# Retention and channel mix on one core: q scaled while it is turned, y copied mostly by ScalarE, 64-token chunks everywhere, a new order

## The chip, the cores and the metric

The kernel runs on one core of one Trainium2 chip. The metric is device time in microseconds (us) of one execution; a result is the median over several runs. The engines are TensorE (PE in the profile; its weight loads are PEld), VectorE (DVE), ScalarE (ACT), GpSimd (POOL) and SyncE (SP); the last three also issue DMAs. Matmuls write PSUM, which has 8 banks of 512 fp32 columns for each of 128 partitions; the other memory on the chip is SBUF.

## What is computed

Two layers, one behind the other. The first is a retention layer over 4 sequences of 768 tokens, with 8 heads of 64 columns; the second mixes each token with the one before it and puts it through two projections and a gate.

```python
gamma = 1.0 - 2.0 ** (-5.0 - np.arange(H))
for t in range(S):
    state = gamma * state + outer(k[t], v[t])        # per batch and head, 64 x 64
    y[t] = (1 / sqrt(D)) * q[t] @ state
...
x = y, heads side by side                            # [4, 768, 512]
xk = mu_k * x + (1 - mu_k) * x_prev
xr = mu_r * x + (1 - mu_r) * x_prev
k = np.maximum(xk @ w_k, 0.0)                        # 512 -> 1024
v = k * k @ w_v                                      # 1024 -> 512
r = sigmoid(xr @ w_r)
out = r * v
```

Inputs and outputs are fp32; the matmuls take fp16.

## The kernel before

The 3,072 tokens are cut into 12 blocks of 256 (three for each sequence). The recurrence is done in chunks: inside a chunk the scores q k are masked and multiplied with v, and what came before the chunk enters through a carried state of 64x64 per head. The powers of gamma are split: `vs` multiplies v by one power as it becomes fp16 (`scale_v`, L280), and the block's y is multiplied by the matching inverse powers, held in the tile `gy`, when it is read from PSUM (`yout`, L573 and L580). `gy` is built on the chip at the start (`powers`).

The work is written out by hand as one long string, `ORDER`: one word for each step, and each engine runs its steps in that order. A word has a code, the block, a part, behind `~` the engine (v VectorE, a ScalarE, p GpSimd, s SyncE) and behind `@` the PSUM banks. In order of the data the codes are:

- `lq`, `lk`, `lv`: loads of a block. Those of GpSimd turn q and k into fp16 on the way. The first heads of block 0 come through SyncE as fp32 and are turned into fp16 by ScalarE (`cq`, `ck`). `wk`, `wr`, `wv` load the weights, `mu` the mixing factors.
- `Tq`, `Tk`: transposes on PE into PSUM; `Eq`, `Ek`: ScalarE copies the transposed blocks to SBUF (L265). For blocks 9 to 11, `tq` and `tk` do both as a transposing DMA on SyncE instead.
- `S`, `M`: scores, and their mask on VectorE (L420). `C`: the chunk's addition to the state; `U`: VectorE adds it to the carried state (L485); `G`: the state decays over to the next block. `I` and `J`: q times the carried state; `Y`: the masked scores times `vs`, into the same banks.
- `D`: y from PSUM to the fp32 tile `xT` (VectorE); `dx`: its difference to the token before (L595); `X`: the two mixes (L621), four column groups each.
- `K`: keys (L635, L645); `Qa`, `Qb`: relu (L667) and square (L675, L679), both on ScalarE; `R`, `s`: gate and sigmoid; `V`: values (L700), in two halves of their sum; `O`: result on VectorE (L706); `st`: store, issued by SyncE. The last half block's values are cut in two (`Vc`, L718; `Oc`, L725).
- `z`: products of zeros on PE, which only fill time at the start.

Attention is done in three ways. Blocks 0 and 1 use chunks of 128 tokens with two tokens interleaved in a row; blocks 2 to 5 (`WIDE`) use chunks of 128 tokens with 128 rows of one chunk; blocks 6 to 11 (`HALF`) use four chunks of 64 tokens, whose products are all 64x64x64, four of them side by side on the array. Blocks 3 to 5 and 9 to 11 load q and k as whole pairs of heads (`PAIRQ`, `PAIRK`), so that one 128x128 transpose turns two heads. Blocks 3 and 4, 6 and 7, 9 and 10 are joint (`GROUPS`): their keys are products of 512 columns (L635), those of the others of 256 (L645).

Tiles come in rings (four of q, k and v; three of `vs`, of the transposed q and k and of the mixes; four of relu outputs), so a step may also wait until a buffer's last reader is done.

## Time and profile before

| what | us |
|---|---|
| runs | 153.79, 364.5, 154.08 |
| median of the runs | 154.08 |
| span of the profiled execution | 152.4 |
| PE busy | 145.3 |
| VectorE busy | 128.0 |
| ScalarE busy | 94.5 |
| GpSimd busy (issuing loads) | 62.1 |

The profile is one execution, taken by the hardware profiler; its span goes from the first to the last instruction, and the execution's own time is somewhat longer: the median of the runs is 1.7 us above this span (the profiled execution's own time isn't among the runs, which are timed without a profile). Durations of single instructions overlap on PE, where the next matmul starts before the last one has ended, so on PE the distance between two starts is the better measure. In a group of instructions the columns are the line, the engine, the operation, output and inputs with shapes, the count, busy time and mean duration in ns, and then the engine's idle time in front of them with what ended it. In a timeline they are the start, the time taken, the engine, the line and the operation.

### The profile page before, as it was taken

The numbers are of one execution on the slowest core, as the hardware profiler recorded it, in microseconds if no ns is written. First come the engines' busy times: TensorE is split into PE (matmuls) and PEld (weight loads), VectorE is DVE, ScalarE is ACT, GpSimd is POOL, SyncE is SP. The second block draws the span as 40 slices with busy tenths as digits, with TensorE's granted clock in tenths as the row PEclk, the third lists the DMA queues.
The fourth block names the chain that finished last, engine by engine and source line by source line (L and its number), as shares of the span: only waits on it lengthen the run. The fifth ranks groups of instructions, "written<-read, shape, count | busy, mean of one in ns | idle before, by whom it ended". The sixth has DMA issues, their size and how long they took to land.

```text
span 152.4 us, 4956 instructions
## 1 busy us (share of the span) xinstructions
PE 145.3 (95%) x2129; PEld 82.4 (54%) x2129; DVE 128.0 (84%) x204; ACT 94.5 (62%) x172; POOL 62.1 (41%) x77
## 2 busy tenths in 40 slices
PE   7969899999999999999999999999999999999991
PEld 3345467657864545545448544447664444466460
DVE  2289999999999999999999998998999999331651
ACT  3655259979955679966418807869450089739430
POOL 7965658999746920599989000000000000000000
PEclk9999999999999999999999999999999999999999
DMA  5999999999999999299999999928103013003153
GB/s 146 237 241 192 181 240 237 148 148 223 167 178 216 213 225 286 68 239 166 258 188 238 236 168 126 152 89 109 38 4 138 0 71 142 0 0 138 69 207 138
DMA packets 56525, 23.83 MB, mean 156 GB/s; under 512 B 48056, under 2 KB 52024, under 8 KB 56504
## 3 DMA queue, kind: packets, MB, share of 16 engines
q0 software_dynamic: 45200, 14.95, 82.1%
q1 hardware_dynamic: 10872, 8.26, 22.3%
q8 instruction: 16, 0.26, 0.7%
q10 hardware_dynamic: 432, 0.32, 0.7%
q14 instruction: 5, 0.04, 0.1%
HBM read 24.31 MB, written 6.29 MB: 201 GB/s over the span
## 4 chain that ended last, share of the span: by engine, by line
PE 73%; DVE 11%; DMA 11%; issue 2%; ACT 0%; DVEq 0%; POOLq 0%
PE ps L700 24%; PE ps L688 14%; PE ps L635 12%; PE ps L645 11%; DMA kT<-k 6%; DMA v<-in_v_dram 5%; DVE a L420 3%; PE ps L507 2%; PE ps L311 2%; DVE xk L621 2%; DVE xT L580 2%; DVE dx L595 2%; PE ps L544 1%; DVE vs L280 1%; PE ps L388 1%
## 5 line engine op out<-in xcount | busy, mean ns | idle before, releaser
L700 PE MATMUL ps<-wv,k2s 128*128 128x512 f16 x184 | 43.9, 380 | 0.0
L667 ACT ACTIVATE kr<-ps 128x512 f32<-128x512 f32 x48 | 27.9, 594 | 23.0 <-PE ps L635 14.9
L700 PEld LDWEIGHTS <-k2s 128*128 128x128 f16 x184 | 17.2, 98 | 19.0
L706 DVE SCALAR_TENSOR_TENSOR os<-ps,rs 128x512 f32<-128x512 f32 x23 | 15.2, 684 | 12.1 <-PE ps L700 6.5
L688 PE MATMUL ps<-wr,xr 128*128 128x512 f16 x96 | 24.0, 379 | 0.0
L259 POOL DMA_DIRECT2D v<-in_v_dram x20 | 18.0, 911 | 13.6 <-DVE vs L280 8.3
L645 PE MATMUL ps<-xk,wk 128*128 128x256 f16 x192 | 23.4, 273 | 0.0
L635 PE MATMUL ps<-xk,wk 128*128 128x512 f16 x96 | 22.8, 379 | 0.0
L420 DVE TENSOR_TENSOR a<-ps,c_sb 128x1024 f16<-128x1024 f32 (+1 forms) x20 | 21.9, 1110 | 0.0
L694 ACT ACTIVATE rs<-ps 128x512 f32<-128x512 f32 x24 | 14.3, 594 | 10.6 <-PE ps L688 8.8
L645 PEld LDWEIGHTS <-wk 128*128 128x128 f16 x192 | 18.2, 98 | 3.9
L621 DVE SCALAR_TENSOR_TENSOR xr<-dx,mu,xT 128x256 f16<-128x256 f32 (+1 forms) x36 | 19.3, 566 | 0.0
L621 DVE SCALAR_TENSOR_TENSOR xk<-dx,mu,xT 128x256 f16<-128x256 f32 (+1 forms) x36 | 18.9, 569 | 0.3
L259 POOL DMA_DIRECT2D k<-in_k_dram x20 | 17.7, 896 | 3.5 <-DMA wv<-in_moe_w_v_dram 1.6
L280 DVE TENSOR_TENSOR vs<-v,csm_sb 128x1024 f16<-128x1024 f32 x12 | 14.5, 1217 | 3.3 <-DMA v<-in_v_dram 3.3
L675 ACT ACTIVATE k2s<-kr 128x512 f16<-128x512 f32 x24 | 14.7, 626 | 0.4
L595 DVE TENSOR_TENSOR dx<-xT 128x1024 f32<-128x1024 f32 x12 | 14.6, 1221 | 0.2
L635 PEld LDWEIGHTS <-wk 128*128 128x128 f16 x96 | 9.1, 98 | 10.5 <-issue 0.2
L679 ACT ACTIVATE k2s<-kr 128x512 f16<-128x512 f32 x24 | 14.5, 625 | 0.3
L688 PEld LDWEIGHTS <-xr 128*128 128x128 f16 x96 | 9.0, 98 | 10.0
L265 ACT COPY qT<-ps 128x1024 f16<-128x1024 f16 (+1 forms) x10 | 9.2, 924 | 7.7 <-PE ps L317 3.7
L265 ACT COPY kT<-ps 128x1024 f16<-128x1024 f16 (+1 forms) x10 | 9.3, 934 | 6.9 <-PE ps L306 3.4
(73 smaller groups left out, 151.3 us busy)
## 6 DMA issues: line engine op xcount, KB each, us to landing
out_dram<-os SPq DMA_DIRECT2D x23, 256.0 KB, 3.8
v<-in_v_dram POOLq DMA_DIRECT2D x20, 256.0 KB, 6.8
k<-in_k_dram POOLq DMA_DIRECT2D x21, 128.0 KB, 6.9
q<-in_q_dram POOLq DMA_DIRECT2D x13, 128.0 KB, 7.1
q<-in_q_dram POOLq DMA_DIRECT2D x5, 256.0 KB, 9.0
v<-in_v_dram POOLq DMA_DIRECT2D x2, 512.0 KB, 7.3
wv<-in_moe_w_v_dram POOLq DMA_DIRECT2D x2, 512.0 KB, 9.5
wk<-in_moe_w_k_dram POOLq DMA_DIRECT2D x2, 256.0 KB, 9.6
```

Source lines behind the costliest of these rows:

```text
L259: e.dma_start(out=to[:, i, hs], in_=src[:, i])
L265: e.copy(out=out, in_=in_)
L280: e.tensor_tensor(out=VS(n), in0=V32(n).rearrange("p (h i d) -> p i h d", i=2, h=H), in1=gks[:, int(half(n) or wide(n)), :, :, None].to_br ...
L420: nc.vector.tensor_tensor(out=dst, in0=dst if n in SPLITM else src, in1=mask[:, None, None, :].to_broadcast(list(dst.shape)), op=ALU.mult,)
L595: e.tensor_tensor(out=DX(k)[:, :, m * TM + t0 : m * TM + t1], in0=x[:, :, c + t0 : c + t1], in1=x[:, :, c - 1 + t0 : c - 1 + t1], op=ALU.s ...
L621: nc.vector.scalar_tensor_tensor(out=XM[w](k)[:, j, t0:t1], in0=DX(k)[:, j, t0:t1], scalar=mu[:, w * NCO + j : w * NCO + j + 1], in1=x[:, ...
L635: nc.tensor.matmul(banks("K", n, g), lhsT=wk16[:, co, g * P : g * P + P], rhs=XM[0](k)[:, co, :], start=(co == 0), stop=(co == NCO - 1),)
L645: nc.tensor.matmul(pz[:, i, :], lhsT=wk16[:, co, fo * P : fo * P + P], rhs=XM[0](k)[:, co, m * TM + t0 : m * TM + t1], start=(i == 0 and c ...
L667: nc.scalar.activation(out=kr, in_=banks("K", n, g, *u), func=AF.Relu)
L688: nc.tensor.matmul(banks("R", n, tb), lhsT=XM[1](k)[:, co, t : t + P], rhs=wr16[:, co, :], start=(co == 0), stop=(co == NCO - 1),)
L700: nc.tensor.matmul(banks("V", n, tb), lhsT=K2(n)[:, fo, tb * P : tb * P + P], rhs=wv16[:, fo, :], start=(fo == 0), stop=(fo == NFO - 1),)
L706: nc.vector.scalar_tensor_tensor(out=OS(2 * n + tb), in0=banks("V", n, tb), scalar=1.0 / (KSC * KSC), in1=RS(2 * n + tb), op0=ALU.mult, op ...
```

## The change

All blocks now use 64-token chunks (`HALF` for all of them; the other two ways and the flags that chose them are gone), so each state has four parts and each block four `U`. The mask has one form. Each k and v is loaded with a chunk's tokens in one row range (two DMAs for each block), each q with two neighbouring tokens in a row. No block is transposed by DMA any more.

The powers of gamma move from y to q: `tu` builds, once, an identity matrix of 64 rows for each head and token parity, scaled by the inverse powers (`scaled_eye`), and q is turned by a matmul with it instead of by a transpose; its PSUM output is fp32 and takes two banks. k is turned by 64x64 transposes. With that, y needs only a constant factor, and `yout` is a copy with a factor: ScalarE does it for most blocks, VectorE for the whole of blocks 5, 8 and 9 and half of blocks 0 and 1. `gy` and `powers` are gone. For seven blocks ScalarE reads two columns of the banks in question (`sy`, `settle`) between `I` and `Y`.

Of 48 squares, 18 go from ScalarE to GpSimd; of 12 scalings of v, 7 go from VectorE to GpSimd, of 12 differences 3 (blocks 3, 7 and 11), and one state decay. The loads of v of blocks 4 to 11 go from GpSimd's queue to SyncE's. The order of all steps is new: at the start, q of block 0 is loaded first on SyncE as before, v of block 0 before the rest of k and q on GpSimd, the first half of `wk` before the second; two of block 0's four key groups come before the scores of block 1, and all but the last half of the values of blocks 0 and 1 come before the transposes of block 3.

```diff
 KSC = 64.0
-KUP = 4.0
-HALF = (6, 7, 8, 9, 10, 11)
-PAIRQ = (3, 4, 5, 9, 10, 11)
-PAIRK = (3, 4, 5, 9, 10, 11)
-WIDE = (2, 3, 4, 5)
-DT = (9, 10, 11)
+YSC = 0.125 * KSC
+DT = ()
...
-gy.0 lq.0.0.2~s lk.0.0.2~s mu~s cq.0.0.2~a lv.0~p z.8@7 Tq.0.0.2@0 ck.0.0.2~a vs.0~v Eq.0.0.2~a
...
+lq.0.0.2~s lk.0.0.2~s lv.0~p mu~s lk.0.2.4~p cq.0.0.2~a tu.0.4~v tu.4.8~v z.11@7 Tq.0.0.2@01
+lq.0.2.4~p ck.0.0.2~a Eq.0.0.2~a z.1@7 Tk.0.0.2@23 lv.1~p Ek.0.0.2~a z.1@7 S.0.0.2@45 M.0.0.2
+lq.1~p vs.0~v z.2@7 mt@6 me~a wk.0 z.1@3 Tk.0.2.4@07 C.0@12 Ek.0.2.4~a U.0.0~v U.0.1~v z.1@6
+Tq.0.2.4@34 lk.1~p U.0.2~v Eq.0.2.4~a U.0.3~v S.0.2.4@56 I.0@07 G.0~a M.0.2.4 sy.0~a wk.1 Y.0
+D.0.1~v D.0.0~a dx.0~v z.2@6 Tq.1@34 Eq.1~a vs.1~p X.0.0.0 X.0.0.3 X.0.0.1 X.0.0.2 wr X.0.1.3
+z.7@6 K.0.0@1 X.0.1.0 X.0.1.2 K.0.1@2 X.0.1.1 Qa.0.0~a lk.2~p Qb.0.0~a C.1@56 Tk.1@07 Qa.0.1~a
+U.1.0~v Ek.1~a U.1.1~v U.1.2~v Qb.0.1~a I.1@34 U.1.3~v S.1@12 G.1~v K.0.2@0 lq.2~p M.1 K.0.3@7
+lv.2~p Qa.0.2~a Y.1 Qa.0.3~a D.1.0~v D.1.1~a R.0.1@5 wv.0 Qb.0.3~a dx.1~v wv.1 R.0.0@6 s.0.1
+Qb.0.2~p X.1.0.3 Tk.2@12 s.0.0 X.1.0.0 Ek.2~a X.1.0.1 lk.3~p X.1.0.2 Tq.2@07 X.1.1.2 K.1.3@3
+X.1.1.3 Eq.2~a X.1.1.0 K.1.1@4 lq.3~p X.1.1.1 Qa.1.3~a R.1.0@5 Qb.1.3~a vs.2~p Qa.1.1~a K.1.0@6
+s.1.0 Qb.1.1~a S.2@12 lv.3~p C.2@07 Qa.1.0~a M.2 K.1.2@3 V.0.1.0@4 U.2.0~v Qa.1.2~a lk.4~p U.2.1~v
+R.1.1@5 Qb.1.2~a U.2.2~v I.2@16 s.1.1 sy.2~a V.0.1.1 lq.4~p Y.2 Qb.1.0~p lv.4~s O.0.1 V.0.0.0@2
...
+Y.11 s.10.1 V.9.1.0@7 D.11~a V.10.1.0@2 dx.11~p V.9.0.0@6 V.10.0.0@0 X.11.1.2 V.9.0.1 X.11.0.2
+X.11.0.3 V.10.1.1 X.11.0.0 O.9.0 V.9.1.1 O.10.1 V.10.0.1 X.11.0.1 st.10.1~s O.9.1 K.11.1@3 O.10.0
...
+    gk_np = gam[None, None, :] ** (C - tok[:, :, None])
+    gq_np = gam[None, None, :] ** (tok_q[:, :, None] - C)
...
+    def scaled_eye(e, h0, h1):
+        hs = slice(h0, h1)
+        e.tensor_tensor(
+            out=turn[:, :, hs], in0=ident[:, None, None, :].to_broadcast([P, 2, h1 - h0, W]),
+            in1=gqs[:, :, hs, None].to_broadcast([P, 2, h1 - h0, W]), op=ALU.mult,
+        )
...
+    def trans_q(e, n, j0=0, j1=NJ):
+        src = held_as(n, 0)
+        pt = turned(n, 0, j0, j1)
+        for j in range(j0, j1):
+            for i in range(2):
+                for u in range(2):
+                    for s, h, hp in heads(j):
+                        nc.tensor.matmul(
+                            pt[low(s), u, j - j0, i], lhsT=src[low(u), i, h],
+                            rhs=turn[low(u), i, h], start=(j == j0 and i == 0),
+                            stop=(j == j1 - 1 and i == 1), skip_group_check=True,
+                        )
...
+    def settle(e, n):
+        copy(e, seen[low(0)], banks("I", n)[low(0), 0, NJ * C - 2 :])
...
-            for v in range(2):
-                nc.vector.tensor_tensor(
-                    out=x[:, :, :, v],
-                    in0=banks("I", n)[:, v].rearrange("p (j i t) -> p j i t", j=NJ, i=2),
-                    in1=g[:, :, :, v], op=ALU.mult,
-                )
+        for u in range(2) if v is None else (v,):
+            if e is nc.scalar:
+                e.activation(out=x[:, u], in_=y[:, u], func=AF.Copy, scale=YSC)
+            else:
+                e.tensor_scalar(out=x[:, u], in0=y[:, u], scalar1=YSC, scalar2=None, op0=ALU.mult)
...
+        if e is nc.scalar:
+            e.activation(out=to, in_=kr, func=AF.Square)
+        else:
+            e.tensor_tensor(out=to, in0=kr, in1=kr, op=ALU.mult)
...
     def store(e, n, tb):
-        nc.sync.dma_start(out=out[b, t0 : t0 + P, :], in_=OS(2 * n + tb))
+        e.dma_start(out=out[b, t0 : t0 + P, :], in_=OS(2 * n + tb))
```

## The prediction

> **What bounds the kernel now.** I read the page's busy times first, then its strip of 40 slices, then the groups by line.

> ```profile
> PE 145.3 (95%) x2129; PEld 82.4 (54%) x2129; DVE 128.0 (84%) x204; ACT 94.5 (62%) x172; POOL 62.1 (41%) x77
> ...
> PE   7969899999999999999999999999999999999991
> ...
> DVE  2289999999999999999999998998999999331651
> ```

> A TensorE (PE) at 95% may be matmuls that wait inside, so I checked it by count: the large projections (keys L645 and L635, gate L688, values L700 and L718), how many there are, and how far apart two of them start in a dense stretch.

> ```profile
> L700 PE MATMUL ps<-wv,k2s 128*128 128x512 f16 x184 | 43.9, 380 | 0.0
> ...
> L688 PE MATMUL ps<-wr,xr 128*128 128x512 f16 x96 | 24.0, 379 | 0.0
> L645 PE MATMUL ps<-xk,wk 128*128 128x256 f16 x192 | 23.4, 273 | 0.0
> L635 PE MATMUL ps<-xk,wk 128*128 128x512 f16 x96 | 22.8, 379 | 0.0
> ```

> ```profile
> 75.27 3.45 PE ps L700 x16
> ...
> 135.16 1.75 PE ps L645 x16
> ...
> 147.29 1.76 PE ps L718 x16
> 149.07 0.42 DVE os L725
> ```

> In the chain of waits, 16 products of 512 columns take 3.45 us (0.2155 each) and 16 of 256 take 1.75 (0.109). So the projections need (184 + 96 + 96) x 0.2155 + (192 + 16) x 0.109 = 81.0 + 22.7 = 103.7 us, and the change alters neither their number nor their shape. The first starts here, in the timeline:

> ```profile
> 20.78 1.09 PE L645 MATMUL ps<-xk,wk 128*128 128x256 f16 x8
> ```

> The last ends at 147.29 + 1.76 = 149.05. Of these 128.3 us, 103.7 are projections; 24.6 are left for all attention products in between and for idleness. To see which, take one run of attention products between projections:

> ```profile
> 69.55 1.03 PE L688 MATMUL ps<-wr,xr 128*128 128x512 f16 x4
> 70.50 0.45 PE L432 MATMUL ps<-vs,k 64*64 64x64 f16 x32
> 70.86 0.45 PE L375 MATMUL ps<-qT,kT 64*64 64x64 f16 x32
> 71.11 0.45 PE L528 MATMUL ps<-a,vs 64*64 64x64 f16 x32
> 71.39 0.32 PE L507 MATMUL ps<-qT,tg 64*64 64x64 f16 x12
> 71.65 1.04 PE L700 MATMUL ps<-wv,k2s 128*128 128x512 f16 x4
> ```

> From 69.55 to 71.65, less 4 x 0.2155, is 1.24 us for 108 products of 64x64x64: 11.5 ns each, the changes to and from the small tiles included. The chain also names a DMA (a transposed load of k, 6% of the span) near 86 us, but that is no hole:

> ```profile
> 86.00:120.00 34.00, 33.57 (x565) 18.22 (x564) 32.18 (x51) 18.20 (x33) 0.00 (x0) 1.00 0.75 103
> ```

> PE is busy 33.57 of those 34.00 us at the full clock. So before 20.78 us VectorE (DVE) and the loads set the pace, and after it PE does, with hardly a gap. The time is: first projection 20.8 + projections 103.7 + small products 24.6 + tail 3.3 (149.1 to the span's end, 152.4) = 152.4. Around the span lies what the runs show beyond it: 154.08 (their median) less 152.4, 1.7 us; the lowest run, 153.79, would make it 1.4. The profiled execution's own time is not among them, so I sum to its span and add 1.7.

> **The change on PE.** From the first projection on, the new order leaves for block 1 all but its q transposes (160 products) and for blocks 2 to 11 all six stages: 5 x 32 + 32 = 192 products each. Less the states and carried terms that first and last blocks of a sequence leave out (32 + 24), that is 2,024 products x 11.5 ns = 23.3 us. Before, the same stretch cost 24.6 with every gap in it. Blocks 2 to 5 get cheaper (16 products with 128 rows or columns become 32 small ones; 8 whole-pair transposes become 32), blocks 9 to 11 get transposes that were DMA transposes before. Turning q by a matmul with a scaled identity, with fp32 output, isn't in the trace; its nearest rows are the 64x64x64 products above, so I keep 11.5 ns. The run above is a long one, and short ones pay the change of tiles more often; so I take the mean of 23.3 and 24.6, 23.9, and keep 23.2 to 25.3 as ends (the upper one if q's products, 22 x 16 of the 2,024, took 15 ns). The new 64-token chunks are thus almost a wash; the time hangs on when the first projection starts (t0) and on the idle time (g) that the new order puts behind it: time = t0 + g + 103.7 + 23.9 + 3.3 + 1.7 = **t0 + g + 132.6**.

> **The change on VectorE, ScalarE, GpSimd.**

> ```profile
> L420 DVE TENSOR_TENSOR a<-ps,c_sb 128x1024 f16<-128x1024 f32 x16 | 19.2, 1217 | 0.0
> ...
> L595 DVE TENSOR_TENSOR dx<-xT 128x1024 f32<-128x1024 f32 x12 | 14.6, 1221 | 0.2
> L280 DVE TENSOR_TENSOR vs<-v,csm_sb 128x1024 f16<-128x1024 f32 x12 | 14.5, 1217 | 3.3 <-DMA v<-in_v_dram 3.3
> ...
> L621 DVE SCALAR_TENSOR_TENSOR xk<-dx,mu,xT 128x256 f16<-128x256 f32 x24 | 10.4, 480 | 0.2
> ...
> L485 DVE TENSOR_TENSOR tg<-ps,tg 128x256 f16<-128x256 f32 x20 | 8.4, 420 | 0.6 <-PE ps L432 0.3
> L573 DVE TENSOR_TENSOR xT<-ps,gy_sb 128x512 f32<-128x512 f32 x12 | 8.3, 689 | 0.7
> ```

> VectorE loses 7 of 12 scalings of v (-8.5 us), five whole masks and two of half size (-7.5), 16 of 24 half-blocks of y (-10: 12 x 0.689 and six whole ones at 1.22, less 8 x 0.689), 3 differences (-3.7) and the short powers of gamma; it gains 15 state sums at 0.42 (+6.3) and two halves of a scaled identity (+1.4, sized like half a copy of y): 128 becomes about 105.

> ```profile
> L667 ACT ACTIVATE kr<-ps 128x512 f32<-128x512 f32 x48 | 27.9, 594 | 23.0 <-PE ps L635 14.9 <-PE ps L645 7.9
> ...
> L675 ACT ACTIVATE k2s<-kr 128x512 f16<-128x512 f32 x24 | 14.7, 626 | 0.4
> ...
> L265 ACT COPY qT<-ps 128x1024 f16<-128x1024 f16 x8 | 8.1, 1010 | 7.2 <-PE ps L306 3.4 <-PE ps L317 3.2 <-PE ps L311 0.6
> ...
> L858 POOL MEMSET const-float32-0.0<- 128x1 f32 x1 | 0.1, 99 | 0.2 <-issue 0.2
> ...
> L750 DVE MEMSET warm<- 128x1 f32 x1 | 0.1, 59 | 0.0
> ```

> ScalarE (ACT) gives 18 squares away (-11.3), takes 16 half-blocks of y (0.59 each by the relu's row, +9.5) and six more transposed copies (+6.1), loses two blocks' state scalings and the powers, and gets seven two-column reads (`sy`) that wait for a block's carried products; behind such a read stand relus, and PE would wait for their banks. About 94.5 + 4.3 = 99 at most, 65% of the span, so I put the hidden cost at nothing (rival 3 prices it without cover).

> GpSimd (POOL) only issues loads now, so the length of its arithmetic is in no row. Below, it is as fast as VectorE (1.22 us for v, 0.6 for a square); the only pair of like rows, two one-column memsets, is 99 against 59 ns, a factor 1.7; I take 2.1 us and 1.1, and three times VectorE (3.7) as the upper end. It gets 7 v, 18 squares, 3 differences and a scaling, 40 to 45 us, and gives 16 loads of v to SP. There they stand behind stores, each of which waits for a result on VectorE; who would wait is the scaling of that block's v, blocks later. I cost that at nothing. [...]

> **t0.** The start is a chain; its steps stand in the timeline:

> ```profile
> 8.30 1.23 DVE L280 TENSOR_TENSOR vs<-v,csm_sb 128x1024 f16<-128x1024 f32 x1 [3.27 <-DMA v<-in_v_dram]
> ...
> 9.57 0.45 PE L461 MATMUL ps<-vs,k 64*64 64x64 f16 x32 [0.27 <-DVE vs L280]
> ...
> 12.84 0.64 PE L555 MATMUL ps<-a,vs 64*64 64x128 f16 x32
> ...
> 13.74 1.22 DVE L580 TENSOR_TENSOR xT<-ps,gy_sb 128x1024 f32<-128x1024 f32 x1
> ...
> 15.00 1.23 DVE L595 TENSOR_TENSOR dx<-xT 128x1024 f32<-128x1024 f32 x1
> ...
> 16.34 0.48 DVE L621 SCALAR_TENSOR_TENSOR xk<-dx,mu,xT 128x256 f16<-128x256 f32 x1
> ```

> Now block 0's difference is ready at 16.2, but block 1's masks and sums come between it and the mixes, so the first projection waits until 20.78. In the new order: v is scaled from about 8.5 (the mask of the first heads goes before it) to 9.7; state 0.45; four sums 1.7, so 11.9; last mask 0.69, 12.6; products to the start of the copy 0.9, 13.5; half a copy 0.69, the other half on ScalarE, 14.2; difference 1.23, 15.5; four mixes at 0.42 (a queue of them runs at that pace), 17.2. PE follows them one by one: **t0 = 17.0**, 3.8 earlier. v now comes in two halves with shorter rows; that may cost up to 1 us or nothing.

> **g.** From there VectorE needs four more mixes (18.9), four sums (20.6), a scaling and mask (22.2), products 0.9 (23.1), half a copy (23.8), difference (25.0), four mixes: 26.7. In these 9.7 us PE has four key groups (8 x 0.109 each: 3.5), two gates (1.7) and 224 small products (160 of block 1, 64 of block 2's transposes: 2.6), 7.8 in all: **1.9 idle**. Next, the second half of wv:

> ```profile
> POOL wk L741 <- DMA q<-in_q_dram: 1.6, 2, 0.8
> ...
> v<-in_v_dram POOLq DMA_DIRECT2D x20, 256.0 KB, 6.8
> ...
> wv<-in_moe_w_v_dram POOLq DMA_DIRECT2D x2, 512.0 KB, 9.5
> ```

> It stands behind 25 loads on GpSimd's queue at some 0.8 us (20), one scaling of v (2.1), and waits of which the quoted one is the longest kind (about 3), from 1.3 on: issued near 26.5, landed at 33.3 with v's 6.8 or at 36 with its own 9.5. PE wants it after two key and gate sets of block 1 (3.5 + 1.7), two stages of block 2 (0.7) and half a value group (0.9): 26.7 + 6.8 = 33.5. So 0 to 2.5 idle; I take **0.5**, nearer to v's, since by then fewer loads queue ahead of it. At the end, block 11's difference is on GpSimd: copy 1.2, difference 2.1, five mixes and two results 3.5, against eight half value groups (32 x 0.2155 = 6.9) on PE: with the steps from engine to engine **0.5** idle. The middle has cover, since VectorE has 23 us less to do; I put 0 there. g = 2.9, and t0 + g + 132.6 = **152.5 us**, 1% under 154.1: t0 + g is 19.9 where it was 20.8, and the small products give 0.7. This case covers 151.2 (v on time, wv free: t0 + g 18.6) to 155.5 (t0 1 us and wv 2 us later).

> **Rivals.** (1) PE is dense from its first projection on: t0 16.3 (v on time, first mixes overlapped), g 1.0: 149.9, 2.7% faster. For it: PE before shows no gaps, and VectorE is eased everywhere. Against: the 1.9 of idle counted above is VectorE's own chain. (2) GpSimd's arithmetic and VectorE's two-input work hold each other up. The place is the start: v of block 1 is due on GpSimd at about 14 to 16, just when the difference and mixes of block 0 run, and a square and v of block 2 at 24 to 30, on the mixes of block 1. If one excludes the other, 2.1 + 1.1 + 2.1 = 5.3 fall on that chain: g 8.2, so 17.0 + 8.2 + 132.6 = 157.8, 2.5% slower; at the upper end of 3.7 for each v it would be 161. It decides once GpSimd takes over 2.5 us for a v or VectorE stands still during it. Of the trace before nothing speaks for or against: GpSimd did no arithmetic. [...] (3) ScalarE in order: a copy of y waits for its products in front of relus that hold PSUM banks, so PE stalls for banks, 0.59 for each of 14 half copies in the middle if nothing covers them, 8 us: 152.5 + 8 = 160.5. That ScalarE stands idle for 38% of the span now, most of it waiting for PE, speaks against it. (4) The change doesn't do what it says, for instance GpSimd's squares come so late that values wait; priced like (3).

> **How the numbers follow.** My case 0.42; rival 1, 0.33; rival 2, 0.17; rivals 3 and 4 together 0.08. What a measurement of this kernel can tell from no change is about 2%, 3.1 us: faster means under 151.0, slower over 157.2. My case lies within; rival 1 is faster; 2 to 4 are slower. The range runs from rival 1 with a little more (149.0: t0 16.0, g 0.4) to rival 2 (157.8).

> **What would show it.** Right: first projection near 17, VectorE at about 104 us busy, GpSimd's v near 2 us, PE idle in 17 to 36 about 3 us and hardly later. Wrong: mixes (0.48) or differences (1.22) that grow longer beside GpSimd's work, PE waiting for relus or for vs after 40 us, or attention products above 11.5 ns each, which at 13 would add 2,024 x 1.5 ns, 3 us.

## The result, and the profile after

The change made the kernel slower: 198.9 us (195.6 to 202.2, 4 runs) against 154.4 beside it, 1.272 times as long (95% interval 1.263 to 1.281). Two of these four runs are slow ones (201.2 and 202.2 us at a mean clock of 0.909 and 0.898, the others 195.6 and 196.5 at 0.925 and 0.939); the ratios to the kernel before, here and below, leave such runs out, so 1.272 is less than the quotient of the two medians. The span of the profiled execution is 194.8 us at a mean clock of 0.939, where it was 152.4 at 1.000. On the page after the change, the busy times and two rows of the strip of 40 slices:

```profile
PE 154.3 (79%) x2845; PEld 85.0 (44%) x2845; DVE 113.4 (58%) x186; ACT 96.9 (50%) x169; POOL 88.6 (46%) x88
...
PE   7576959389976837978677766799789988799991
...
PEclk9955888859999999999999999699999999999999
```

TensorE (PE) has holes from end to end, and its granted clock is a half from 10.4 to 20.7 us and again from 27.5 to 30.9, 37.7 to 44.6 and 123.1 to 126.5. To see where the time went, I gave each matmul the time to the next one's start, less the idle time that the trace lists in front of the next one (0.15 us and over). For the kernel before, the change, and four of the kernels below:

| us | first projection | idle after it | projections | small products, filling zeros | last matmul starts |
|---|---|---|---|---|---|
| before | 20.8 | 0.6 | 106.6 | 20.8 | 148.8 |
| after | 21.6 | 29.9 | 115.1 | 23.9 | 190.5 |
| e1_again | 23.2 | 14.2 | 110.8 | 24.3 | 172.5 |
| e8_spread | 22.4 | 13.0 | 110.2 | 23.5 | 169.2 |
| e12_loads | 21.5 | 13.3 | 111.4 | 25.9 | 172.1 |
| e14_vs_v | 19.7 | 6.3 | 110.5 | 29.5 | 166.0 |

Of the 41.7 us between before and after, 29.3 are PE waiting, 8.5 are projections (some 5 of them because 42 ran at half the clock), 3.1 small products and 0.8 the later start. What PE waited for, from the list of waits of the change (total, times, longest):

```profile
PE ps L507 <- DVE a L333: 5.1, 3, 2.2
PE ps L465 <- DVE xk L445: 3.1, 2, 2.7
PE ps L465 <- ACT qT L233: 2.6, 2, 1.5
PE ps L455 <- ACT kr L477: 2.4, 2, 1.2
PE ps L291 <- ACT k L233: 2.3, 1, 2.3
PE ps L507 <- ACT qT L233: 2.2, 2, 1.1
```

Values (L507) need no mask `a` and no `qT`, and keys (L465) no `qT`. Of these six only the waits for the mixes `xk` and for the late `k` are for data that the step reads; the relu `kr` may hold a bank that the keys need. Over the whole trace, keys, gates and values wait eleven times, 14.6 us in all, for a mask or for a copy of `qT` or `kT`, none of which they read. One wait of the odd kind in the timelines of ScalarE, VectorE and PE:

```profile
24.84 1.01 ACT L233 COPY kT<-ps 128x1024 f16<-128x1024 f16 x1
```

```profile
24.32 0.42 DVE L361 TENSOR_TENSOR tg<-ps,tg 128x256 f16<-128x256 f32 x1 [0.58 <-PE ps L344]
25.88 0.88 DVE L361 TENSOR_TENSOR tg<-ps,tg 128x256 f16<-128x256 f32 x2 [1.13 <-ACT kT L233]
```

```profile
23.83 0.45 PE L344 MATMUL ps<-vs,k 64*64 64x64 f16 x32
24.10 0.46 PE L291 MATMUL ps<-c_sb,k 64*64 64x64 f16 x32
25.90 0.22 PE L385 MATMUL ps<-qT,tg 64*64 64x64 f16 x2 [1.33 <-ACT kT L233]
```

VectorE's second sum of block 1 (`U.1.1`) reads bank 6, one of the pair 5 and 6; ScalarE's copy of `kT` (`Ek.1`) reads banks 0 and 7 (`C.1@56`, `Tk.1@07` in the order). They share nothing, and yet the sum waits until that copy ends, and PE behind it. The copy takes its two banks in one instruction with a stride of seven banks. In the kernel before every pair is of neighbours (01, 23, 45, 67); in the new order many are not (07, 16, 36, 57, 14, 27). My theory F: an instruction that reads a pair is ordered by the program's semaphores against every instruction on the banks from the first of the pair to the last, reads included. The eleven waits fit it: each time the waiting step's bank lies between the two of the step that it waits for. The three values that wait for a mask, for example, are `V.4.0.0@2`, `V.5.1.0@4` and `V.6.0.0@5`, and the masks read `S.10@17`, `S.8@17` and `S.9@46`.

### The profile page after: what moved, and what is told of

The parts are those of the page before. It is cut to its first block, busy times and chain, and to the rows that moved or that the text cites. A ratio compares the mean times of both kernels' runs of the same rounds, so it can differ in the third digit from the quotient of the medians.

```text
span 194.8 us, 6385 instructions
## 1 busy us (share of the span) xinstructions
PE 154.3 (79%) x2845; PEld 85.0 (44%) x2845; DVE 113.4 (58%) x186; ACT 96.9 (50%) x169; POOL 88.6 (46%) x88
## 3 DMA queue, kind: packets, MB, share of 16 engines
q1 hardware_dynamic: 21704, 10.89, 20.8%
## 4 chain that ended last, share of the span: by engine, by line
PE 56%; DVE 20%; ACT 14%; issue 4%; DMA 3%; SPq 0%; DVEq 0%; ACTq 0%
PE ps L507 15%; PE ps L465 11%; PE ps L495 9%; PE ps L455 8%; DVE a L333 5%; DVE xk L445 5%; ACT kT L233 4%; DMA k2s<-in_k_dram 3%; ACT qT L233 3%; DVE dx L436 3%; DVE xr L445 3%; ACT kr L477 3%; PE ps L408 2%; PE ps L385 2%; ACT xT L426 2%
## 5 line engine op out<-in xcount | busy, mean ns | idle before, releaser
L507 PE MATMUL ps<-wv,k2s 128*128 128x512 f16 x184 | 44.4, 385 | 9.2 <-DVE a L333 5.1
L489 POOL TENSOR_TENSOR k2s<-kr 128x512 f16<-128x512 f32 x18 | 19.6, 1094 | 67.2 <-ACT kr L477 67.2
L477 ACT ACTIVATE kr<-ps 128x512 f32<-128x512 f32 x48 | 27.5, 594 | 37.4 <-PE ps L465 24.0
L465 PE MATMUL ps<-xk,wk 128*128 128x256 f16 x192 | 28.0, 298 | 6.0 <-DVE xk L445 3.1
L507 PEld LDWEIGHTS <-k2s 128*128 128x128 f16 x184 | 17.3, 98 | 28.5 <-issue 9.7
L445 DVE SCALAR_TENSOR_TENSOR xr<-dx,mu,xT 128x256 f16<-128x256 f32 (+1 forms) x36 | 22.6, 667 | 11.0 <-POOL dx L436 11.0
L455 PE MATMUL ps<-xk,wk 128*128 128x512 f16 x96 | 22.7, 379 | 4.6 <-ACT kr L477 2.4
L465 PEld LDWEIGHTS <-wk 128*128 128x128 f16 x192 | 19.9, 106 | 13.1 <-issue 8.0
L333 DVE TENSOR_TENSOR a<-ps,c_sb 128x1024 f16<-128x1024 f32 (+1 forms) x13 | 14.8, 1141 | 16.9 <-PE ps L322 11.6
L227 POOL DMA_DIRECT2D k<-in_k_dram x24 | 21.4, 902 | 5.0 <-PE ps L344 4.7
L445 DVE SCALAR_TENSOR_TENSOR xk<-dx,mu,xT 128x256 f16<-128x256 f32 (+1 forms) x36 | 20.6, 615 | 2.0 <-POOL dx L436 1.8
L233 ACT CAST qT<-ps 128x1024 f16<-128x1024 f32 (+1 forms) x13 | 12.3, 944 | 17.1 <-PE ps L278 5.4
L361 DVE TENSOR_TENSOR tg<-ps,tg 128x256 f16<-128x256 f32 x32 | 13.5, 421 | 10.0 <-ACT kr L477 5.1
L487 ACT ACTIVATE k2s<-kr 128x512 f16<-128x512 f32 x30 | 18.9, 629 | 0.8
L251 POOL TENSOR_TENSOR vs<-v,csm_sb 128x1024 f16<-128x1024 f32 x7 | 14.7, 2103 | 8.5 <-issue 8.4
L436 DVE TENSOR_TENSOR dx<-xT 128x1024 f32<-128x1024 f32 x9 | 11.0, 1231 | 5.3 <-ACT xT L426 5.3
## 6 DMA issues: line engine op xcount, KB each, us to landing
out_dram<-os SPq DMA_DIRECT2D x23, 256.0 KB, 2.2
v<-in_v_dram SPq DMA_DIRECT2D x16, 256.0 KB, 7.8
q<-in_q_dram POOLq DMA_DIRECT2D x11, 256.0 KB, 5.5
k<-in_k_dram POOLq DMA_DIRECT2D x22, 128.0 KB, 5.9
v<-in_v_dram POOLq DMA_DIRECT2D x8, 256.0 KB, 6.1
wv<-in_moe_w_v_dram POOLq DMA_DIRECT2D x2, 512.0 KB, 9.7
wk<-in_moe_w_k_dram POOLq DMA_DIRECT2D x2, 256.0 KB, 7.6
wk<-in_moe_w_k_dram POOLq DMA_DIRECT2D x4, 128.0 KB, 7.5
```

The source lines that it names most:

```text
L227: e.dma_start(out=to[:, i, hs], in_=src[:, i])
L233: e.copy(out=out, in_=in_)
L333: nc.vector.tensor_tensor(out=dst, in0=src, in1=step[:, None, None, :].to_broadcast(list(dst.shape)), op=ALU.mult,)
L436: e.tensor_tensor(out=DX(k)[:, :, m * TM : m * TM + TM], in0=x[:, :, c : c + TM], in1=x[:, :, c - 1 : c - 1 + TM], op=ALU.subtract,)
L445: nc.vector.scalar_tensor_tensor(out=XM[w](k)[:, j, 0:wide], in0=DX(k)[:, j, 0:wide], scalar=mu[:, w * NCO + j : w * NCO + j + 1], in1=x[: ...
L455: nc.tensor.matmul(banks("K", n, g), lhsT=wk16[:, co, g * P : g * P + P], rhs=XM[0](k)[:, co, m * TM : m * TM + 2 * TM], start=(co == 0), ...
```

## The experiments

The theories beside F were G (GpSimd's arithmetic holds VectorE and the products that need it) and O (the new order puts real waits in PE's way).

**Pairs cut.** e1_split is the change with the three steps that read a pair cut into one instruction for each bank; nothing else differs.

```diff
-        copy(e, to.rearrange("c j u (p i) -> c u j p i", i=2), pt.rearrange(...))
+        for u in range(2):
+            copy(e, to.rearrange(...)[:, u], pt.rearrange(...)[:, u])
...
-        nc.vector.tensor_tensor(out=dst, in0=src, in1=step...)
+        for a in range(2):
+            nc.vector.tensor_tensor(out=dst[:, a], in0=src[:, a], in1=step...)
```

> The changed kernel, with each ScalarE or VectorE step that reads a pair of PSUM banks (Eq, Ek, M) cut into two instructions, one for each bank; nothing else is changed, and the steps keep their order. Theory F (a read of two banks that are not neighbours is ordered against every bank between them, so steps wait that share no data): most of the 44 us goes, to 158 to 168 us, and the 1 us waits of U and K for Eq and Ek are gone. Theory G (GpSimd's arithmetic and VectorE's two-input work exclude each other): stays above 188. Theory O (the order itself: real data and a late k at the start): stays above 185.

177.2 us (175.4, 178.9); the same kernel run again as e1_again gives 178.8, 1.154 of before. By the ratios (1.272 to 1.154) some 18 us go with the cut, by far the largest piece that any edit took off; less than I had expected of F alone. The three sums now run in one stretch, released by PE's products alone (timeline of e1_again), and of the eleven waits of keys, gates and values for masks and copies one is left, of 0.9 us:

```profile
25.54 1.41 DVE L365 TENSOR_TENSOR tg<-ps,tg 128x256 f16<-128x256 f32 x3 [1.90 <-PE ps L348]
```

**Pairs spread in the kernel before.** e2_before_apart renames the banks of the kernel before so that each pair stands four apart (01 becomes 04, 23 becomes 15, and so on); the order and every instruction stay.

```diff
-        b = BANK[key]
+        b = [(0, 4, 1, 5, 2, 6, 3, 7)[x] for x in BANK[key]]
```

> The kernel before, with its eight PSUM banks renamed so that each pair that it reads in one instruction lies four banks apart (0 and 4, 1 and 5, 2 and 6, 3 and 7) instead of side by side; the work and the order are the same. Theory F: slower by 20 us or more, over 174 us, with waits of steps on banks that they do not share. Theories G and O: no change, 153 to 156.

211.4 us (209.2, 213.7): the faster run is 55 over the kernel before, by a change of names. The masks themselves take no longer (1.22 us in both kernels), so reading banks that stand apart is not slow in itself. Waits of the same kind appear:

```profile
PE ps L507 <- DVE a L420: 5.0, 4, 1.5
PE ps L388 <- DVE a L420: 4.6, 3, 2.0
PE ps L700 <- DVE a L420: 4.5, 1, 4.5
```

F is shown from both sides; it explains some 18 of the 42 us by which the change is slower. What makes up the rest is asked below.

**GpSimd's arithmetic.** e3_no_gpsimd is the change with its 29 arithmetic steps of GpSimd back on VectorE (scalings, differences, decay) and ScalarE (squares); e4_split_no_gpsimd does the same to e1_split.

```diff
-vs.1~p ... dx.3~p ... G.9~p ... Qb.0.2~p ...
+vs.1~v ... dx.3~v ... G.9~v ... Qb.0.2~a ...
```

> The changed kernel with GpSimd's 29 arithmetic steps put back at the same places of the order: 7 scalings of v, 3 differences and 1 decay on VectorE, 18 squares on ScalarE. Theory F: between 185 and 200, since the false waits stay. Theory G: 160 to 175, and the mixes at 0.48 us again. Theory O: no change within 5.

> Both edits together: bank pairs read in two instructions, and no arithmetic on GpSimd. Theory F with some G: 154 to 162, less than either alone. Theory O: above 180, as the order is the same.

195.7 us, 1.270 of before (1.258 to 1.281) where the change has 1.272, and 178.7 (177.1, 180.4): worth nothing that can be told from noise, with the pairs or without them. The second missed both forecasts: what is left beside the pairs is not G. G is not the cause of the slowdown; what it is worth comes out further down, when other waits no longer cover it.

**What is left of e1_split.** e1_again repeats it beside three variants.

> The kernel of e1_split once more, as the base of the three runs beside it: 177 us (175.4 to 178.9 so far) under every theory. It stands 23 us above the kernel before. By its trace I put these down to: 8.9 us of pauses of TensorE which no semaphore ends and which all stand at one place in the count of its weight loads and matmuls (numbers 701, 955, 1723, 1979, 2235, 3257, 5049 and 5307, all 185 to 189 above a multiple of 256; 256 instructions are what one 16,384-byte packet of the instruction queue holds at 64 bytes); 5.6 us of waits for data; 13.7 us after the first projection at half the clock, worth about 6.8; and a first projection at 21.49 that only looks like before's 20.78, since it was to be at 17.0.

178.8 us, 1.154 of before (1.144 to 1.164). The number 5307 was wrongly on my list: it waits for a mix; the others sum to 8.6 us, and to 7.6 in this trace. What a packet holds can be counted on the change, whose page has 22 packets of 16,384 bytes on the instruction queue (packets, MB, share of the 16 DMA engines):

```profile
q8 instruction: 22, 0.36, 0.7%
```

Its 5,690 weight loads and matmuls pass a number that is 187 above a multiple of 256 just 22 times (in the kernel before, 16 packets and 16 times). So 256 to a packet, 64 bytes each, is an estimate from these counts. e5_start, e6_shift and e7_fill differ from it in the order alone:

```diff
 e5_start
-lq.0.0.2~s lk.0.0.2~s ... S.0.0.2@45 M.0.0.2 lq.1~p vs.0~v ... G.0~a M.0.2.4 sy.0~a
+lk.0.0.2~s lq.0.0.2~a ... S.0.0.2@45 vs.0~v lq.1~p M.0.0.2 ... sy.0~a G.0~a M.0.2.4
 e6_shift (n: matmuls of zeros of 64x64)
-z.1@7 Tk.0.0.2@23
+z.1@7 n.64@7 Tk.0.0.2@23
 e7_fill
-X.1.1.2 K.1.3@3
+X.1.1.2 z.8@3 K.1.3@3
```

> e1_split with the start reordered: k of the first heads is asked for first, on SyncE, and q on ScalarE's queue; v of block 0 is scaled ahead of the first mask; the small settling copy stands ahead of the decay on ScalarE. Theory T (the late first k holds the start: its cast stands at 8.13 against 5.03 before, and TensorE waits 2.67 for it): cast at 5.0 to 6.5, first projection at 18 to 19.7, time 2 to 4 us under e1_again. Rival (the start is set by VectorE's chain or by the half clock from 7.6 to 21.3 whatever k does): first projection 20.8 to 21.6 and no change within 1 us.

176.4 us, 1.145 (1.138 to 1.153). The first k was cast at 7.2 (8.8 in e1_again), now right behind the cast of q, whose load on ScalarE's queue kept it until 6.7; and the first projection came at 21.5: PE was at half the clock from 7.7, and 3.0 us of zeros stood ahead of it. The rival's reading of the start, then; a gain of 1 to 2 us that the two intervals do not tell from none.

> e1_split with 64 matmuls of zeros of 64x64 (128 more PE instructions with their weight loads) put where TensorE idles for the first k, so that they cost no time there (0.74 us in a gap of 2.67). Theory N (TensorE starves for its own instructions at the end of each packet of 256): the pauses move in the program by 128 instructions and stay at 185 to 189 above a multiple of 256; the long one, 3.67 us in the middle of block 5's k transposes, comes 64 products earlier, among the carried products and scores of block 4, at about 63 to 65 us if the rest runs alike. Rival W (these products wait for a load or a copy which the profile does not name): the pauses stay ahead of the same products of block 5 and their number is now 57 to 61 above a multiple of 256. Time 174 to 181 by both.

181.6 us, 1.177 (1.173 to 1.181, two runs): a little over the 174 to 181 of both readings and 3 us over e1_again, though its first projection came 2.9 us earlier, at 20.3; PE's idle time behind that is 18.6 us where e1_again has 14.2. The long pause in the timelines of PE, first e1_again, then e6_shift:

```profile
70.06 0.53 PE L291 MATMUL ps<-c_sb,k 64*64 64x64 f16 x24 [4.77 <-issue]
```

```profile
66.90 0.31 PE L389 MATMUL ps<-qT,tg 64*64 64x64 f16 x4 [5.97 <-issue]
```

Counted over weight loads and matmuls it stands at number 2235 in both, 187 above a multiple of 256, but 64 products earlier in the program: ahead of block 4's carried products in place of block 5's transposes. So PE does not wait for data there; I read "issue" here as PE without instructions, at the end of a packet of 256. The packets of 16,384 bytes are in the trace: in e1_again the one that ends this pause is fetched at 67.2, 4.7 us after the last one was opened, at 62.5.

> e1_split with 8 fp16-sized passes of zero matmuls (1.7 us at full clock) ahead of block 1's first key projection, where TensorE idles 2.35 us for the mixes. Theory C (the granted clock falls to a half for the 3.4-us windows that follow a window with idle time): the half clock from 34.95 to 41.78 is gone or one window long, time 1.5 to 3.5 us under e1_again. Rival (the clock falls for another reason): the half clock stays, and the time is the same or up to 1.7 us longer.

177.7 us, 1.153 (1.147 to 1.158), within e1_again's interval, so no gain in time is shown: the half clock from 36.8 is gone, but the one of the start lasted to 25.2 in place of 23.2, so behind the first projection it is 10.1 us against 10.4. In these two runs the clock follows the idle time. In windows of the two kernels (length; busy of PE, PEld, VectorE, ScalarE, GpSimd; granted clock, DMA share, GB/s), first e1_again:

```profile
33.40:36.80 3.40, 0.83 (x26) 0.55 (x26) 3.37 (x5) 1.55 (x4) 3.40 (x3) 1.00 1.79 155
36.80:40.30 3.50, 3.38 (x16) 2.16 (x15) 1.74 (x5) 1.33 (x3) 3.13 (x4) 0.51 1.19 202
```

```profile
33.40:36.80 3.40, 2.37 (x29) 1.11 (x29) 3.37 (x4) 2.16 (x5) 3.40 (x3) 1.00 1.88 163
36.80:40.30 3.50, 3.25 (x24) 2.23 (x24) 2.25 (x6) 1.90 (x4) 3.50 (x5) 1.00 1.11 196
```

With PE busy 0.83 of 3.4 us the next 3.4 us run at half; with 2.37 they do not. A window that was a quarter busy, then, did not keep the full clock. The other traces say the same. The half clock of the change lasts 10.2, 3.4, 6.8 and 3.4 us, one to three steps of 3.4 each time; cut into such steps, the 18 traces have 53 steps at full clock with PE busy for less than half of the step, and 51 of them are followed by a step at half clock. Of 75 steps with PE busy for a half to three quarters 6 are, and of 667 busier ones none.

**Spreading the small products, and all repairs together.** e8_spread moves two groups of values into the densest run of small products; e9_all adds the other repairs.

```diff
 e8_spread
-Y.4 vs.5~v s.2.0 Tk.5@35 Tq.5@26 D.4~a dx.3~p V.2.1.0@7 Ek.5~a dx.4~v Tk.6@01 V.2.0.0@4
+Y.4 vs.5~v s.2.0 D.4~a V.2.1.0@7 V.2.0.0@4 Tk.5@35 Tq.5@26 dx.3~p Ek.5~a dx.4~v Tk.6@01
 e9_all, besides
-lk.0.0.2~s / z.11@7 / z.1@7 Tk.0.0.2 / vs.2~p / dx.3~p / K.1.3@3
+lk.0.0.2~a / z.14@7 / z.6@7 Tk.0.0.2 / vs.2~v / dx.3~v / z.6@3 K.1.3@3   (lv.2 and vs.2 also earlier; and e5_start's other moves)
```

> e1_split with two groups of 8 value projections of block 2 (3.4 us of TensorE) moved ahead of the turning products of block 5, into the run of small products in which TensorE consumes a packet of 256 instructions in 2.8 us while the next one's fetch starts 3.9 us after the last was opened. Theory N (it is the density of instructions: long projections let the fetch catch up): the pause of 3.67 (4.77 in the second look) at number 2235 is gone or under 1 us, the half clock that followed it (6.8 us) too, time 3 to 6 us under e1_again's 178.84, 173 to 176. Rival (the pause belongs to these loads and copies, or the moved projections are missed later as cover for the mixes of blocks 3 and 4): 177 to 180, with waits for mixes in place of the pause.

> e8_spread and all the other repairs together: the first k on ScalarE's queue, zeros that fill the wait for it, v of block 0 ahead of the first mask and the settling copy ahead of the decay; block 2's v and block 3's differences on VectorE, zeros ahead of block 1's first key projection. If the price beside the bank pairs is these four things (start, fetch, clock, GpSimd beside the mixes), each repaired once: first projection 18.5 to 20, time 164 to 171. If the order itself (what stands ahead of what) holds the rest: not under 172, with new waits for data behind those taken away.

175.5 us, 1.137 (1.135 to 1.140), and 177.6, 1.148 (1.140 to 1.156). In e8_spread the pause at number 2235 fell from 4.8 to 1.9 and the half clock behind it is gone, but the next packet's end took 1.6 us. e9_all missed: its pause at that packet came back at 4.2 us, one of 1.75 appeared at number 443 ahead of the first projection (21.6), and no new waits for data came.

**Fewer PE instructions, and the loads of v.** e10_pair turns k in 8 products a block in place of 32; e11_pair_start adds most of the start of e9_all and takes the differences of blocks 3 and 11 back to VectorE; e12_loads and e13_loads_start are these two with the loads of v of blocks 4 to 11 issued by GpSimd.

```diff
 e10_pair
-                    for s, h, hp in heads(j):
-                        nc.tensor.transpose(pt[low(s), u, j - j0, i], src[low(u), i, h], ident[low(u)])
+                nc.tensor.transpose(pt[:, j - j0, i], src[:, i, 2 * j : 2 * j + 2]..., eye)
 e12_loads, e13_loads_start
-lv.4~s ... lv.11~s
+lv.4~p ... lv.11~p
```

> e8_spread with k turned as in most blocks of the kernel before: 8 transposes of 128x128 a block into one bank in place of 32 of 64x64 into two, and one copy of 128x1024 out of it; 288 products and their weight loads fewer, 5,114 PE instructions in place of 5,690. Theory N (TensorE starves for instructions in dense runs of small products): the pauses, 8.3 us together in e8_spread, fall to 5 or less, and with 1.4 us less of small products the time is 4 to 7 us under 175.5, 168 to 172. Rival (the number of instructions costs only its own execution): 1 to 2 us under, 173.5 to 174.5, pauses as before.

> e10_pair with the start of e5_start and e9_all, but for the queue of the first k, which stays: zeros of 1.1 us more for the wait for k and of 1 matmul-second less ahead of the first key projection (3 short passes in place of 1 long and 3 short), v of block 0 and the settling copy earlier; zeros ahead of block 1's first key projection; the differences of blocks 3 and 11 on VectorE. First projection 19.5 to 21 if zeros at half clock held it (22.4 in e8_spread), 21.5 to 22.5 if the mixes do; time 2 to 4 us under e10_pair, or no change.

> e10_pair with the loads of v of blocks 4 to 11 issued by GpSimd in place of SyncE, at the same places of the order, so that they go out one behind the other with those of q and k. If the bursts on SyncE's queue (four transfers of 256 KB asked for at 57.4 to 65.2) hold up the instruction packets (opened at 58.38, fetched 4.1 us later): the pause of 3.58 near 65 us falls under 1, the half clock from 64.6 goes, time 3 to 6 us under 174.4. Rival (any load does it, or the number of instructions): pause 3 to 4, time within 1.5 us of 174.4, or up to 4 us longer where GpSimd's squares now stand behind loads.

> e11_pair_start with the same loads on GpSimd: as e12_loads against its own base of 174.25, 168 to 171 if SyncE's bursts hold up the packets, 173 to 178 if not.

e10_pair 174.4 us, 1.131 (1.126 to 1.136); e11_pair_start 174.3, 1.127 (1.121 to 1.133), its first projection at 18.5, earlier than either reading had it, with no gain in time. The pauses at packets' ends fell as N says (7.5 us in e8_spread, not the 8.3 I had put; 5.0 in e10_pair), the time only as the rival says: a 128x128 transpose is dearer than I took it (67 ns from start to start, 0.53 us for the 8 of a block, where 32 small ones take 0.37), so the small products grew to 25.4 us. The longest pause stayed, now ahead of values, while SyncE issued four loads of v. First PE's row, then SyncE's; the v that the first names is only the landing nearest in time, since values read no v:

```profile
64.83 1.89 PE L509 MATMUL ps<-wv,k2s 128*128 128x512 f16 x4 [3.58 <-DMA v<-in_v_dram]
```

```profile
57.38 7.80 SPq L228 DMA_DIRECT2D v<-in_v_dram x4
```

e12_loads 177.7 us, 1.148 (1.141 to 1.154); e13_loads_start 176.1, 1.140 (1.137 to 1.143). The pauses fell (2.0 us in e12_loads), the long one to nothing there: the fetch for that packet, which had started 4.1 us after the last one was opened, starts 0.6 us after it (4.4 in e11_pair_start, 1.4 in e13_loads_start). At this place, then, the burst of loads on SyncE's queue held up the packet; but it need not be that queue, for in e14_vs_v below, with these loads on GpSimd, one fetch again starts 4.1 us late. The time went up all the same, for PE now waits for mixes (e12_loads, list of waits), and these stand beside GpSimd (timelines of its VectorE and GpSimd):

```profile
PE ps L467 <- DVE xk L447: 5.4, 2, 3.4
PE ps L497 <- DVE xr L447: 2.8, 2, 2.3
```

```profile
31.99 3.19 DVE L447 SCALAR_TENSOR_TENSOR xk<-dx,mu,xT 128x256 f16<-128x256 f32 x4
```

```profile
31.42 2.29 POOL L252 TENSOR_TENSOR vs<-v,csm_sb 128x1024 f16<-128x1024 f32 x1
```

**GpSimd's arithmetic once more.** e14_vs_v is e13_loads_start with GpSimd's seven scalings, last difference and decay (9 steps) back on VectorE, while its loads stay, and so asks which of the two lengthens the mixes; e15_no_p takes the 18 squares to ScalarE as well.

> e13_loads_start with the seven scalings of v, one difference and one decay of GpSimd back on VectorE (9 steps); squares stay on GpSimd. [...]

> e14_vs_v with the 18 squares of GpSimd on ScalarE as well, so that GpSimd only issues loads. [...]

171.0 us, 1.102 (1.096 to 1.109), and 172.2, 1.112 (1.106 to 1.119). Against e13_loads_start's 1.140 the first is worth 5 to 6 us; the squares cost nothing where they were (in the change 1.09 us each on GpSimd, 0.63 on ScalarE). The same four mixes now take 1.67, though GpSimd issues loads beside them (from 31.57), so it is its arithmetic that stretched them:

```profile
32.19 1.67 DVE L447 SCALAR_TENSOR_TENSOR xk<-dx,mu,xT 128x256 f16<-128x256 f32 x4
```

Nothing tried beats the kernel before: e14_vs_v, the fastest of the repaired ones, stays 16 us over it. By the table its waits (6.3 us) are no longer the main part; the small products, its filling zeros and the stretches at half clock are. What a new order for the 64-token products could reach was not tried.

## Why the prediction was wrong

The forecast was 152.5 us with a range to 157.8, and even 25% for slower stopped at 160.5. By its steps:

- **g, the idle time: "The middle has cover, since VectorE has 23 us less to do; I put 0 there."** This is the step that failed. g was 2.9 in the sum and 29.9 on the chip, 22.8 of it between 36 and 125 us, in the middle that was to have cover. VectorE indeed did less (113.4 us from 128.0), but cover by busy time says nothing about who is ordered behind whom. I read the new order for what each step computes and not for the banks that it names; the copy with `@07` held up a sum on bank 6 for 1.13 us. e1_split (-18 us) and e2_before_apart (+55 us) show what such waits are worth. No rival had this mechanism.
- **The 103.7 us of projections at full clock.** They took 115.1, before 106.6 by the same count. The sum had the clock at 1.00 as in the trace before, where PE was never idle for long; the idle time that I put at 0 brought the half clock with it (13.7 us of it after the first projection).
- **"The change on PE": instructions.** 23.9 us for the small products was right (23.9; 2,024 of them, as counted, at 11.8 ns). The 24.6 that it was set against was not: that remainder also held the 0.6 of idle time and the 2.9 that the projections take beyond 103.7. By one count the products went from 20.8 to 23.9, so they cost 3.1 us more, where the sum had them give 0.7. That 716 more matmuls are also 1,432 more instructions to bring in had no term. In the change itself this is small (2.3 us at packets' ends, since PE is slow for other reasons); with the pairs cut it is 7.6 to 8.6 us.
- **t0 = 17.0.** It was 21.6. "v now comes in two halves with shorter rows; that may cost up to 1 us or nothing" looked at the wrong load: k of the first heads, too, came in two halves, was cast at 8.6 (5.0 before), and everything behind it moved; then "half a copy 0.69, the other half on ScalarE" went one after the other (ScalarE's half waits for VectorE's, which writes the same tile):

```profile
18.59 0.60 ACT L426 ACTIVATE xT<-ps 128x512 f32<-128x512 f32 x1 [1.69 <-DVE xT L428]
```

- **"The change on VectorE, ScalarE, GpSimd".** GpSimd's durations were right: 2.1 and 1.1 us forecast, 2.10 and 1.09 measured; so was ScalarE's sum (99 at most, 96.9). VectorE's was 8 too low, 5.0 of it the mixes (43.2 us on the page, 38.2 before), which stretch beside GpSimd's arithmetic (24 of them, of `xk`, took 695 ns each in e13_loads_start and 478 in e14_vs_v). In the change:

```profile
L489 POOL TENSOR_TENSOR k2s<-kr 128x512 f16<-128x512 f32 x18 | 19.6, 1094 | 67.2 <-ACT kr L477 67.2
L251 POOL TENSOR_TENSOR vs<-v,csm_sb 128x1024 f16<-128x1024 f32 x7 | 14.7, 2103 | 8.5 <-issue 8.4
```

```profile
L445 DVE SCALAR_TENSOR_TENSOR xr<-dx,mu,xT 128x256 f16<-128x256 f32 x24 | 13.3, 596 | 11.0 <-POOL dx L436 11.0
L445 DVE SCALAR_TENSOR_TENSOR xk<-dx,mu,xT 128x256 f16<-128x256 f32 x24 | 12.2, 550 | 0.1
```

- **Rival 2** had a mechanism that is there, in the wrong place in the queue: it is worth nothing while other waits cover it (e3_no_gpsimd, e4_split_no_gpsimd) and 5 to 6 us when they are gone (e14_vs_v). That its price was 5.3 us is chance: that was two scalings and a square at the start, this is nine steps over the whole kernel, and the squares cost nothing. No run shows by what the two engines hold each other up; shown are the four mixes, 3.19 us beside GpSimd's scaling and 1.67 without it. **Rival 3**, ScalarE in order, did not come as put: ScalarE is idle half the time, and PE waits for relus only 2.4 us (`kr` in the list of waits).

Of the cause, shown are the pairs, the packets' ends, the clock behind idle time, the burst of loads at the longest pause and GpSimd's arithmetic beside the mixes. Not separated is how the 16 us of e14_vs_v divide among half clock, small products and the order's own waits, nor was the first k tried with the longer rows of the kernel before.

## What to carry to other kernels

Read bank numbers like data: here steps that read two PSUM banks by a strided view held up steps on the banks between (18 us of the change, 55 us in e2_before_apart), so keep pairs neighbours or give each bank its own instruction. Before counting on busy time as cover, ask of every step what is ordered behind it; and when a change cuts matmuls smaller, count instructions as well as columns (7.6 us at packets' ends in e1_again). Causes cover one another: an edit that was worth nothing beside larger waits (e3_no_gpsimd, 1.270 against 1.272) was worth 5 to 6 us, with nine of its 29 steps, once they were gone (e14_vs_v), so try it again.
